# Attention, a routed mixture of experts and a dense layer on one core: the order of the products in the experts' second layer

## The chip, the cores and the metric

The kernel runs on one core of a Trainium2 chip. The metric is the device time of one execution in microseconds (us). The kernel before was timed in three runs; one more execution was taken by the hardware profiler.

## What is computed

Causal attention with a window of 64 positions over 4 batches, 8 heads, 576 positions and a head dimension of 64 gives N = 2304 tokens of 512 columns. A routed layer follows, and then a dense one:

```
skip_score = x @ w_skip;  do_compute = skip_score > 0
xc = x[do_compute]; e_idx = argmax(xc @ w_gate); gate_w = softmax(...)[e_idx]
for e in range(8):
    h = maximum(xc[e_idx == e] @ w1[e], 0)          # 512 -> 1024
    y[e_idx == e] = gate_w * (h @ w2[e])            # 1024 -> 512
out[do_compute] = xc + y
h2 = out @ w_in                                      # 512 -> 2048
g  = 0 if h2 <= -1 else h2 if h2 >= 1 else (h2+1)**2/4
return g @ w_out                                     # 2048 -> 512
```

## The kernel before

All products of the two layers are split products. A float32 operand v is kept as an upper half (ScalarE, ACT, rounds a copy) and a lower half (VectorE, DVE, subtracts the copy from v), and one product a*b becomes three matmuls: upper by upper, upper by lower, lower by upper. `PASSES = ((0, 0), (0, 1), (1, 0))` names the halves of the stationary and of the moving operand. The function `split` (lines 116 to 118) makes the halves of an activation: line 117 is ACT's upper half, line 118 DVE's lower half, which needs line 117 first. `split_pair` (lines 120 to 125) does the same for 1024 columns of weights, line 122 on ACT and line 123 on DVE.

Three stages follow each other: attention with the routing (to about 147 us of the span), the experts (to about 313 us), and the dense layer. The change touches the experts.

The expert stage works through the 8 experts in order. Expert e takes its tokens in tiles of 128 rows, gathered from the DRAM tile x1 by an indirect DMA that GpSimd (POOL) issues (`load_x`, line 650) and scattered back in the same way (`store_x`, line 657). The first tile of each expert is always computed; a second, a third and more only if the count of the expert asks for it (the branches of lines 774, 779 and 783). `prep` transposes a tile on TensorE (PE, line 665, four transposes) and splits it into mxT. `ffn` then does, for one tile:

- the first layer in two halves of 512 inner columns, `mm1` into the banks ha and hb (line 682). `mm1` has 12 products for a half, its 8 products with the upper half of mxT first, its 4 with the lower half last;
- `evac` (ACT, line 689) takes a half out of PSUM with the relu, `tr` transposes it on PE (line 695, four transposes into hTp) and splits it into hT. The first half's `tr` stands in the middle of hb's products;
- the second layer, 24 products into one bank y (line 720), 12 with the first half of the inner columns (j = 0), 12 with the second (j = 1). The second half's `tr` stands after the sixth of j = 0;
- line 726 on DVE: y times the gate plus the tile.

Within one j the kernel before goes over the four blocks c of 128 inner columns and does the three products of a block one after the other:

```
for c in range(4):
    ...
    for a, b in PASSES:
        nc.tensor.matmul(
            py, lhsT=hT[j][:, a, c, :], rhs=halves[4 * e + 2 + j, c][:, b, :],
```

so the third product of a half (c = 0, a = 1) is the first that reads the lower half of hT.

The weights of the next experts are loaded (SyncE's queue) and split while an expert is computed. Where this stands in the program is set by the hooks of `ffn` (lines 761 to 772): at "start", "a", "b" and before each block of j = 1 the function `work` issues the next weight splits, and hook 0 prepares the first tile of the next expert. So ACT and DVE have weight splits between the splits of mxT and hT, in the order of the program, and an engine takes its instructions in that order. POOL's queue alternates between gathers for later tiles and scatters of finished ones; both go to x1, and each scatter stands behind the gathers ahead of it and each gather behind the scatters ahead of it. The dense layer loads its rows from x1 after the last scatter; between the last tile and these rows PE does 28 matmuls whose results are not used (`keep_warm`, line 946).

Of the kernel before, what the change touches and what calls it, by code (L numbers as in the profile page):

```python
# [60 lines left out]
PASSES = ((0, 0), (0, 1), (1, 0))  # L61
# [3 lines left out]
def moe_chain(  # L65
# [10 lines left out]
    nc = tc.nc  # L76
# [11 lines left out]
    halves = {}  # L88
# [27 lines left out]
    def split(dst_hi, dst_lo, src):  # L116
        nc.scalar.activation(dst_hi, src, AF.Copy)  # L117
        nc.vector.tensor_tensor(dst_lo, src, dst_hi.bitcast(F32), ALU.subtract)  # L118
# [129 lines left out]
    with ExitStack() as actx:  # L248
# [308 lines left out]
        for t in range(NT):  # L557
# [19 lines left out]
            if t >= 5:  # L577
                t0, i, n, side = of[t - 5]
# [19 lines left out]
        t1, n = NT - ROUTES[-1], ROUTES[-1]  # L598
# [42 lines left out]
    with ExitStack() as ectx:  # L641
# [3 lines left out]
        def bank(i, shape, name):  # L645
            return psp.tile(shape, F32, tag=f"bank{i}", name=name)
# [23 lines left out]
        def ffn(e, x, xT, name, hooks=(), b0=0):  # L670

            hooks = dict(hooks)

            def at(k):
                if k in hooks:
                    hooks[k]()

            def mm1(ph, j, lo, hi):
                seq = [(c, a, b) for p in (PASSES[:2], PASSES[2:]) for c in range(KD) for a, b in p]
                for n in range(lo, hi):  # L680
                    c, a, b = seq[n]
                    nc.tensor.matmul(  # L682
                        ph, lhsT=xT[:, a, c, :], rhs=halves[4 * e + j, c][:, b, :],
                        start=(n == 0), stop=(n == len(seq) - 1),
                    )

            def evac(ph, j):
                h = mp.tile([P, 512], F32, tag="h", name=f"h{name}_{j}")
                nc.scalar.activation(h, ph, AF.Relu)
                return h  # L690

            def tr(h, j):
                pt = bank(b0 + j, [P, 4, P], f"hTp{name}_{j}")
                for c in range(4):
                    nc.tensor.transpose(pt[:, c, :], h[:, c * P : (c + 1) * P], ident)
                hT = mp.tile([P, 2, 4, P], F32R, tag=f"hT{j}", name=f"hT{name}_{j}", bufs=1)
                split(hT[:, 0], hT[:, 1], pt)
                return hT

            at("start")  # L700
            pa = bank(b0, [P, 512], f"ha{name}")
            mm1(pa, 0, 0, 12)
            ha = evac(pa, 0)
            pb = bank(b0 + 1, [P, 512], f"hb{name}")
            mm1(pb, 1, 0, 6)
            hTa = tr(ha, 0)
            at("a")
            mm1(pb, 1, 6, 12)
            hb = evac(pb, 1)
            py = bank(b0 + 2, [P, 512], f"y{name}")  # L710
            hT = [hTa, None]
            for j in range(2):
                for c in range(4):
                    if j == 0 and c == 2:
                        hT[1] = tr(hb, 1)
                        at("b")
                    if j == 1:
                        at(c)
                    for a, b in PASSES:
                        nc.tensor.matmul(  # L720
                            py, lhsT=hT[j][:, a, c, :], rhs=halves[4 * e + 2 + j, c][:, b, :],
                            start=(j == 0 and c == 0 and (a, b) == PASSES[0]),
                            stop=(j == 1 and c == 3 and (a, b) == PASSES[-1]),
                        )
            y = x[:, 0:DM]
            nc.vector.scalar_tensor_tensor(y, py, x[:, DM:RW], y, op0=ALU.mult, op1=ALU.add)

# [11 lines left out]
        def tile_of(e, t, hooks=()):  # L739
            ffn(e, xe[e, t], xeT[e, t], f"{e}_{t}", hooks, 4 if t else 0)  # L740
# [10 lines left out]
        for e in range(NE):  # L751
# [22 lines left out]
            with tc.If(counts[e] > P):  # L774
                pre(e, 1)
                fetch(e, 2)
                tile_of(e, 1)
                store_x(at_of(e, 1), xe[e, 1])
                with tc.If(counts[e] > 2 * P):  # L779
                    pre(e, 2)  # L780
                    tile_of(e, 2)
                    store_x(at_of(e, 2), xe[e, 2])
                    with tc.If(counts[e] > 3 * P):
                        with tc.For_i(0, (counts[e] - (2 * P + 1)) // P, 1) as i:
                            at = mp.tile([P, 1], I32, tag="at", name=f"at{e}", bufs=1)
                            nc.vector.tensor_copy(at, idx[:, bass.ds(i + (e * NT + 3), 1)])
                            x = load_x(at, f"{e}_l", "mxl", 1)
                            ffn(e, x, prep(x, f"{e}_l", "mxTl"), f"{e}_l", b0=4)
                            store_x(at, x)
# [282 lines left out]
```

## Time and profile before

| what | us |
|---|---|
| median of 3 runs | 749.52 |
| lowest and highest of the 3 | 745.4, 752.06 |
| the profiled execution | 744.33 |
| its span, first to last instruction | 742.6 |
| time of the profiled execution outside of the span | 1.73 |

The mean granted clock of TensorE over the span is 0.98 of full speed. Times in the rows below are us from the start of the span. PE is TensorE's matmul, PEld its weight load, DVE VectorE, ACT ScalarE, POOL GpSimd. The ends of matmuls are modelled: two matmuls that follow each other overlap in the rows, so the distance from one start to the next is the better measure.

### The profile page before, as it was taken

To read this page: it belongs to the slowest core of one execution; us is meant where nothing else is said; L and a number is where in the kernel's file an instruction comes from. 1 tells how busy PE (TensorE), PEld (TensorE's weight loads), DVE (VectorE), ACT (ScalarE), POOL (GpSimd) and SP (SyncE) were. 2 spreads that over 40 slices of the span, in tenths; PEclk is the share of its full clock that TensorE was granted. 3 is DMA by queue.
4 is the path that set the end of the run, shared out by engine and by line. 5 is a ranking of instruction groups with operands and counts; after the bars stand their busy time and mean duration, and the time that the engine had idled before them with its cause. 6 is when DMAs were issued, how large, how long until landed. Compare 5 with 4: busy or idle time off the path is not lost.

```text
span 742.6 us, 12124 instructions
## 1 busy us (share of the span) xinstructions
PE 682.9 (92%) x4605; PEld 581.4 (78%) x4605; DVE 432.9 (58%) x851; ACT 382.3 (51%) x761; POOL 95.1 (13%) x96
## 2 busy tenths in 40 slices
PE   7677887789798999799899999999999999999997
PEld 6565666667676777488798998999998998998995
DVE  4477776649759159679888874434343443333332
ACT  5654663027456257356676665545444544445443
POOL 2335554322022122100000000000000000000000
PEclk9987999999999999999999999999999999999999
DMA  8896965158949348354242400202030021002001
GB/s 262 261 280 199 288 197 144 31 172 265 334 134 350 115 126 297 135 172 142 87 142 86 128 1 0 72 15 72 15 86 1 1 44 43 1 0 44 1 1 43
DMA packets 34502, 88.81 MB, mean 120 GB/s; under 512 B 6958, under 2 KB 8110, under 8 KB 34420
## 3 DMA queue, kind: packets, MB, share of 16 engines
q1 hardware_dynamic: 26208, 74.34, 32.5%
q10 hardware_dynamic: 5892, 6.83, 2.8%
q0 software_dynamic: 2320, 6.58, 2.7%
q8 instruction: 47, 0.77, 0.4%
q14 instruction: 35, 0.29, 0.1%
HBM read 75.65 MB, written 13.12 MB: 120 GB/s over the span
## 4 chain that ended last, share of the span: by engine, by line
PE 47%; DVE 7%; DMA 3%; issue 2%; ACT 2%; ACTq 0%; POOLq 0%; DVEq 0%; SPq 0%
PE po L862 23%; PE h L833 23%; DVE c L855 2%; DMA x<-mx,idx 2%; ACT q L845 1%; DVE gs L853 1%; DVE w L123 1%; DVE c L852 1%; PE p2x L824 1%; DMA mx<-x,idx 1%; DVE q L844 1%; DVE x2T L118 0%; DVE q L848 0%; PE spare L946 0%; DVE c_first L855 0%
## 5 line engine op out<-in xcount | busy, mean ns | idle before, releaser
L833 PE MATMUL h<-x2T,w 128*128 128x384 f32 x1152 | 218.2, 337 | 4.3 <-ACT x2T L117 2.2
L862 PE MATMUL po<-w,gs 128*128 128x512 f32 x864 | 217.4, 395 | 0.7 <-DVE w L123 0.6
L833 PEld LDWEIGHTS h<-x2T,w 128*128 128x128 f32 x1152 | 204.6, 188 | 13.6 <-DVE x2T L118 2.7
L862 PEld LDWEIGHTS po<-w,gs 128*128 128x128 f32 x864 | 159.5, 188 | 31.2 <-DVE w L123 1.3
L841 ACT ACTIVATE q<-h 128x384 f32<-128x384 f32 x96 | 47.0, 489 | 109.7 <-PE h L833 108.3
L844 DVE TENSOR_SCALAR q<-q 128x384 f32<-128x384 f32 x96 | 34.3, 358 | 99.9 <-ACT q L841 99.6
L848 DVE TENSOR_TENSOR q<-hs,q 128x384 f32<-128x384 f32 x96 | 53.6, 559 | 49.5 <-ACT q L845 49.5
L850 ACT ACTIVATE gs<-q 128x384 fp32r<-128x384 f32 x96 | 50.4, 525 | 60.0 <-DVE q L848 60.0
L853 DVE TENSOR_TENSOR gs<-q,gs 128x384 fp32r<-128x384 f32 x96 | 53.6, 558 | 43.8 <-ACT gs L850 43.8
L720 PE MATMUL y<-w,hT 128*128 128x512 f32 x264 | 69.3, 402 | 4.9 <-DVE hT L118 4.9
L122 ACT ACTIVATE w<-raw 128x1024 fp32r<-128x1024 f32 x64 | 65.4, 1063 | 14.1 <-PEq L779 3.6
L845 ACT ACTIVATE q<-q 128x384 f32<-128x384 f32 x96 | 50.5, 526 | 23.3 <-DVE q L844 20.1
L720 PEld LDWEIGHTS y<-w,hT 128*128 128x128 f32 x264 | 47.7, 188 | 17.4 <-DVE hT L118 8.4
L123 DVE TENSOR_TENSOR w<-raw,w 128x1024 fp32r<-128x1024 f32 x50 | 58.9, 1218 | 2.6 <-ACT w L122 1.6
L323 ACT ACTIVATE pr<-s,nb 128x128 f32<-128x128 f32 x144 | 39.1, 386 | 29.4 <-DVE nb L319 29.4
L843 ACT ACTIVATE hs<-h 128x384 f32<-128x384 f32 x96 | 46.8, 488 | 0.0
L123 POOL TENSOR_TENSOR w<-raw,w 128x1024 fp32r<-128x1024 f32 x14 | 33.4, 2387 | 62.1 <-ACT w L122 62.1
L682 PE MATMUL ha<-w,mxT 128*128 128x512 f32 x132 | 34.0, 404 | 7.8 <-DVE mxT L118 3.3
L348 PE MATMUL o<-vt,pts 128*64 128x65 f32 x576 | 27.0, 250 | 12.4 <-DMA vt<-in_vs 11.1
L682 PEld LDWEIGHTS ha<-w,mxT 128*128 128x128 f32 x132 | 23.8, 188 | 17.1 <-DVE mxT L118 4.1
L348 PEld LDWEIGHTS o<-vt,pts 128*64 128x64 f32 x576 | 23.6, 160 | 16.3 <-DMA vt<-in_vs 10.8
L682 PE MATMUL hb<-w,mxT 128*128 128x512 f32 x132 | 35.0, 401 | 0.0
(159 smaller groups left out, 702.4 us busy)
## 6 DMA issues: line engine op xcount, KB each, us to landing
raw<-in_wu SPq DMA_DIRECT2D x62, 512.0 KB, 6.4
raw<-in_wd SPq DMA_DIRECT2D x32, 512.0 KB, 4.3
x<-x SPq DMA_DIRECT2D x20, 256.0 KB, 3.3
x<-x ACTq DMA_DIRECT2D x19, 256.0 KB, 5.8
vt<-in_vs SPq DMA_DIRECT2D x36, 130.0 KB, 5.6
out<-out SPq DMA_DIRECT2D x36, 128.0 KB, 2.4
q<-in_qs SPq DMA_DIRECT2D x8, 512.0 KB, 7.4
kt<-in_ks SPq DMA_DIRECT2D x8, 512.0 KB, 8.4
```

What stands on the lines that cost most here:

```text
L122: nc.scalar.activation(t[:, 0], src, AF.Copy)
L123: eng.tensor_tensor(t[:, 1], src, t[:, 0].bitcast(F32), ALU.subtract)
L348: nc.tensor.matmul(o[k * BLK : (k + 1) * BLK, h, 0:VW], lhsT=pts[k][:, h // 2, half * BLK : (half + 1) * BLK], rhs=vt[(2 * t + k) % B][:, ...
L682: nc.tensor.matmul(ph, lhsT=xT[:, a, c, :], rhs=halves[4 * e + j, c][:, b, :], start=(n == 0), stop=(n == len(seq) - 1),)
L720: nc.tensor.matmul(py, lhsT=hT[j][:, a, c, :], rhs=halves[4 * e + 2 + j, c][:, b, :], start=(j == 0 and c == 0 and (a, b) == PASSES[0]), s ...
L833: nc.tensor.matmul(ph, lhsT=halves[U_IN + m // 4, c][:, b, (m % 4) * P : (m % 4 + 1) * P], rhs=xT[:, a, c, :], start=(n == 0), stop=(n == ...
L841: nc.scalar.activation(q, ph, AF.Relu, bias=0.5, scale=0.5)
L845: nc.scalar.activation(q, q, AF.Square)
L848: nc.vector.tensor_tensor(q, h, q, ALU.max)
L850: nc.scalar.activation(gs[:, 0], q, AF.Copy)
L853: dve.tensor_tensor(gs[:, 1], q, gs[:, 0].bitcast(F32), ALU.subtract)
L862: nc.tensor.matmul(po[i], lhsT=gs[:, a, i * P : (i + 1) * P], rhs=w[:, b, :], start=(m == m0 and (a, b) == PASSES[0]), stop=(m == m1 - 1 a ...
```

## The change

In each half j the 12 products are put in the order that `mm1` has: first the 8 with the upper half of hT (a = 0) for c = 0 to 3, then the 4 with its lower half (a = 1). The second half's `tr` and hook "b" stay after the sixth product of j = 0, and the hooks 0 to 3 after the same numbers of products of j = 1 as before. The products, their operands and their sum are the same.

```diff
             hT = [hTa, None]
+
+            seq = [(c, a, b) for p in (PASSES[:2], PASSES[2:]) for c in range(4) for a, b in p]
             for j in range(2):
-                for c in range(4):
-                    if j == 0 and c == 2:
+                for n, (c, a, b) in enumerate(seq):
+                    if j == 0 and n == 6:
                         hT[1] = tr(hb, 1)
                         at("b")
-                    if j == 1:
-                        at(c)
-                    for a, b in PASSES:
-                        nc.tensor.matmul(
-                            py, lhsT=hT[j][:, a, c, :], rhs=halves[4 * e + 2 + j, c][:, b, :],
-                            start=(j == 0 and c == 0 and (a, b) == PASSES[0]),
-                            stop=(j == 1 and c == 3 and (a, b) == PASSES[-1]),
-                        )
+                    if j == 1 and n % 3 == 0:
+                        at(n // 3)
+                    nc.tensor.matmul(
+                        py, lhsT=hT[j][:, a, c, :], rhs=halves[4 * e + 2 + j, c][:, b, :],
+                        start=(j == 0 and n == 0), stop=(j == 1 and n == len(seq) - 1),
+                    )
```

On PE, the second layer of the first tile of expert 2 (hT_0_0 is the first half of the inner columns, hT_0_1 the second; w_0 and w_2 are weight tiles with the blocks c = 0, 1 and c = 2, 3; mpx is the next expert's tile that hook 0 prepares). Before:

```order
L720 MATMUL y_0_3411<-w_0_3034,hT_0_0_3385 128x512 x6
L695 MATMUL hTp_0_1_3418<-ident,h_0_1_3409 128x128 x4
L720 MATMUL y_0_3411<-w_2_3042,hT_0_0_3385 128x512 x6
L665 MATMUL mpx_0_3442<-ident,mx_0_2919 128x128 x4
L720 MATMUL y_0_3411<-w_0_3348,hT_0_1_3423 128x512 x6
L720 MATMUL y_0_3411<-w_2_3353,hT_0_1_3423 128x512 x6
```

With the change, the same place on PE:

```order
L721 MATMUL y_0_3411<-w_0_3034,hT_0_0_3385 128x512 x4
L721 MATMUL y_0_3411<-w_2_3042,hT_0_0_3385 128x512 x2
L695 MATMUL hTp_0_1_3418<-ident,h_0_1_3409 128x128 x4
L721 MATMUL y_0_3411<-w_2_3042,hT_0_0_3385 128x512 x2
L721 MATMUL y_0_3411<-w_0_3034,hT_0_0_3385 128x512 x2
L721 MATMUL y_0_3411<-w_2_3042,hT_0_0_3385 128x512 x2
L665 MATMUL mpx_0_3442<-ident,mx_0_2919 128x128 x4
L721 MATMUL y_0_3411<-w_0_3348,hT_0_1_3423 128x512 x4
L721 MATMUL y_0_3411<-w_2_3353,hT_0_1_3423 128x512 x4
L721 MATMUL y_0_3411<-w_0_3348,hT_0_1_3423 128x512 x2
L721 MATMUL y_0_3411<-w_2_3353,hT_0_1_3423 128x512 x2
```

The transposes of lines 695 and 665 stand after the same number of products as before; only the products of one half have changed places, so that the last four of each half are those with hT's lower half.

On DVE, the same tile, from the lower half of the second hT (line 118, hT_0_1) to the first layer of the expert's second tile (mxT_1). These rows are the same before and with the change, as are all rows of DVE, ACT, POOL and SyncE:

```order
L118 TENSOR_TENSOR hT_0_1_3423<-hTp_0_1_3418,hT_0_1_3423 128x512
L123 TENSOR_TENSOR w_2_3426<-raw_2_3010,w_2_3426 128x1024
L123 TENSOR_TENSOR w_0_3431<-raw_0_3032,w_0_3431 128x1024
L118 TENSOR_TENSOR mxT_0_3447<-mpx_0_3442,mxT_0_3447 128x512
L123 TENSOR_TENSOR w_2_3453<-raw_2_3037,w_2_3453 128x1024
L123 TENSOR_TENSOR w_0_3458<-raw_0_3045,w_0_3458 128x1024
L123 TENSOR_TENSOR w_2_3466<-raw_2_3351,w_2_3466 128x1024
L726 SCALAR_TENSOR_TENSOR mx_0_2451<-y_0_3411,mx_0_2451 128x512
L774 COMPARE_AND_BRANCH
L118 TENSOR_TENSOR mxT_1_3484<-mpx_1_3479,mxT_1_3484 128x512
```

Nothing moves here: five weight splits, mxT of the next expert and line 726 stand between the lower half of hT_0_1 and the lower half of mxT_1 in both kernels.

## Rows read from the trace of the kernel before

**Rows 1.** The page: the span, and busy time of each engine.
```profile
span 742.6 us, 12124 instructions
PE 682.9 (92%) x4605; PEld 581.4 (78%) x4605; DVE 432.9 (58%) x851; ACT 382.3 (51%) x761; POOL 95.1 (13%) x96
```
**Rows 2.** The page's groups: count, then busy us, mean ns, idle before.
```profile
L720 PE MATMUL y<-w,hT 128*128 128x512 f32 x264 | 69.3, 402 | 4.9 <-DVE hT L118 4.9
```
**Rows 3.** Waits from 150 to 312 us: total, times, longest.
```profile
PE y L720 <- DVE hT L118: 4.9, 8, 0.9
```
**Rows 4.** Timeline of PE at expert 2: start, us, instruction, idle before it.
```profile
184.87 0.62 PE L720 MATMUL y<-w,hT 128*128 128x512 f32 x2
186.13 1.20 PE L720 MATMUL y<-w,hT 128*128 128x512 f32 x4 [0.64 <-DVE hT L118]
...
189.35 0.72 PE L720 MATMUL y<-w,hT 128*128 128x512 f32 x2
190.92 2.57 PE L720 MATMUL y<-w,hT 128*128 128x512 f32 x10 [0.85 <-DVE hT L118]
...
194.61 2.12 PE L682 MATMUL ha<-w,mxT 128*128 128x512 f32 x8 [0.69 <-ACT mxT L117]
198.45 0.72 PE L682 MATMUL ha<-w,mxT 128*128 128x512 f32 x2 [1.72 <-DVE mxT L118]
```
**Rows 5.** Timeline of DVE in the same stretch.
```profile
185.39 0.68 DVE L118 TENSOR_TENSOR hT<-hTp,hT 128x512 fp32r<-128x512 f32 x1
...
190.18 0.68 DVE L118 TENSOR_TENSOR hT<-hTp,hT 128x512 fp32r<-128x512 f32 x1
...
197.72 0.68 DVE L118 TENSOR_TENSOR mxT<-mpx,mxT 128x512 fp32r<-128x512 f32 x1
```
**Rows 6.** Two stretches: length, busy us and instructions of each engine, PEclk, DMA share, GB/s.
```profile
169.57:198.40 28.83, 24.27 (x114) 18.30 (x112) 27.29 (x33) 18.91 (x24) 4.63 (x4) 1.00 0.90 310
219.33:241.40 22.07, 18.57 (x84) 13.66 (x82) 21.74 (x25) 14.91 (x19) 5.43 (x4) 1.00 0.92 322
```
**Rows 7.** Timeline of PE at the second tile of expert 4.
```profile
241.44 1.20 PE L682 MATMUL ha<-w,mxT 128*128 128x512 f32 x4 [1.55 <-DVE mxT L118]
```
**Rows 8.** Timeline of PE at experts 6 and 7: two sets of 12 products.
```profile
279.26 3.04 PE L682 MATMUL ha<-w,mxT 128*128 128x512 f32 x12
...
289.85 3.01 PE L720 MATMUL y<-w,hT 128*128 128x512 f32 x12
```
**Rows 9.** DMA issues from 283.5 to 285 us: the gather of 283.87, us to landing.
```profile
mx<-x,idx POOLq DMA_INDIRECT x1, 8.2
```
**Rows 10.** The chain that ended last, from 292 us: start, us, what.
```profile
292.89 6.62 DMA x<-mx,idx
...
300.44 4.62 DMA mx<-x,idx
...
305.84 3.37 DMA x<-mx,idx
...
310.12 2.66 DMA x<-mx,idx
```
**Rows 11.** Timeline of DVE: line 726 of the last tile.
```profile
306.01 0.75 DVE L726 SCALAR_TENSOR_TENSOR mx<-y,mx 128x512 f32<-128x512 f32 x1 [0.16 <-PE y L720]
```
**Rows 12.** Timeline of PE in attention, and at the start of the dense layer.
```profile
53.00 0.33 PE L348 MATMUL o<-vt,pts 128*64 128x65 f32 x2 [1.88 <-DMA vt<-in_vs]
...
54.73 1.97 PE L333 MATMUL pt<-ident,pr 128*128 128x128 f32 x8
...
61.63 1.09 PE L333 MATMUL pt<-ident,pr 128*128 128x128 f32 x8
...
315.99 0.30 PE L824 MATMUL p2x<-ident,x 128*128 128x128 f32 x1 [2.82 <-DMA x<-x]
```
**Rows 13.** Stretches, columns as in rows 6.
```profile
54.38:57.79 3.41, 3.41 (x27) 2.39 (x27) 1.75 (x4) 0.60 (x1) 1.96 (x1) 0.50 1.04 314
...
194.32:201.15 6.83, 4.82 (x21) 3.65 (x22) 4.07 (x5) 0.84 (x2) 0.00 (x0) 1.00 0.95 310
...
317.20:320.61 3.41, 3.41 (x13) 1.92 (x12) 2.55 (x4) 2.40 (x4) 0.00 (x0) 0.50 0.75 259
```

## The prediction

> **What bounds the kernel now.** I read the page first, then the groups and the waits of the expert stage, then the timelines of PE, DVE and POOL through it, and at last the chain that ended last. PE is the busiest engine by far [rows 1], but the share is an average over three stages, and the change touches only the expert stage. There the changed line has 264 products, 24 for each of 11 computed tiles, and PE's idle time just before them is 4.9 us [rows 2]. All of it is eight waits for the lower half of hT, the longest 0.9 us [rows 3]. So at most eight of 22 halves wait at all.
>
> The reader should then look at who is late. At expert 2 PE does two products, waits for line 118, and does the rest; this happens in both halves, and further on the first layer of the expert's second tile waits 1.72 us, again for line 118 [rows 4]. DVE's rows show why: the lower halves of hT start at 185.39 and 190.18 with no idle time before them, and the lower half of mxT at 197.72 has none either [rows 5]. DVE is busy for 27.29 of 28.83 us from 169.57 to 198.40, and for 21.74 of 22.07 us from 219.33 to 241.40 [rows 6]; it is working off weight splits. PE is released from the second stretch in the same way, after 1.55 us, at 241.44 [rows 7]. In these two stretches DVE sets the time, not the order of PE's products.
>
> The end of the stage is set by something else again. From 292.89 the chain that ended last is scatter, gather, scatter, scatter, one after the other [rows 10]. The scatter at 292.89 stands behind the gather issued at 283.87, which lands 8.2 us later, at 292.07 [rows 9]. The last tile is finished by DVE at 306.01 + 0.75 = 306.76 [rows 11], but its scatter starts only at 310.12 [rows 10]: the tile lies there for 3.4 us because the scatter before it has not landed.
>
> **What the change does to PE, step by step.** The pitch of the products: 12 of them take 3.01 us [rows 8] with a mean of 0.402 us for one [rows 2], so (3.01 - 0.40) / 11 = 0.24 us from start to start. Before, the lower half had to be there after two products, 0.48 us into a half. Now it has eight, 1.9 us, and for j = 0 also the four transposes in between.
>
> What each wait costs PE by starts: at j = 1 of expert 2 it is 190.92 - 189.35 - 0.48 = 1.09 us where the row says 0.85, at j = 0 it is 186.13 - 184.87 - 0.48 = 0.78 where it says 0.64 [rows 4]. The modelled end of a product hides 0.14 to 0.24 us, so the eight waits are worth about 4.9 + 8 x 0.19 = 6.4 us of PE's time. Taken alone each is shorter than the 1.4 us of new slack, so as long as nothing else moves, they all go.
>
> The price of the new order itself: line 682 already works in this order, and its 12 products take 3.04 us against 3.01 us in the old order [rows 8]. The bounds are thus 0 and 22 x 0.03 = 0.7 us; a gain from the order alone is excluded, since products, shapes and operands stay. I take 0. No DMA, no split and no wait of another engine is moved, so nothing has to be costed on the queues of ACT, DVE, POOL and SyncE.
>
> What of the 6.4 us reaches the end:
>
> (The parts are counted by starts, as above, and add up to 6.4.)
>
> - Expert 1's second half and both halves of expert 2 hold three of the waits, 0.8 + 0.8 + 1.1 = 2.7 us. They lie in the stretch in which DVE never rests, and its order is unchanged, so the lower half of mxT still comes at 197.72 + 0.68 = 198.40 and PE goes on at 198.45. Gain: 0. Since PE now comes early to j = 1, it still waits there until 190.9, but with four products behind it instead of ten; so it arrives 6 x 0.24 = 1.4 us earlier at the first layer of the second tile, and the wait of 1.72 us becomes about 3.2 us.
> - Two of expert 4's waits, 1.5 us, lie in the second such stretch. Gain: 0. The 1.55 us at 241.44 grow by 0.7 us (ACT's weight splits let no more through) to the full 1.5 us; I take 2.3 us.
> - The last three, 2.2 us at experts 5 to 7, come after DVE's queue has drained, so PE does get ahead. But the scatters do not: the tile is ready 1.5 to 2.2 us earlier and lies 5 to 5.6 us instead of 3.4. Gain: 0, with bounds of -1.3 us (if the scatter at 292.89 waits for DVE's split that ends just there, and not for the gather) and +0.5 us (weight loads that start earlier beside a scatter).
>
> So the sum by work is 0, and what is left is PE's clock. In rows at 0.50 the engine had been idle shortly before: 1.88 us idle at 53.00 [rows 12], then the stretch from 54.38 at 0.50, the lower level of 1.2 GHz [rows 13]; 2.82 us idle at 315.99 [rows 12], then 317.20 to 320.61 at 0.50 [rows 13]. The wait of 1.72 us at expert 2 was not followed by a fall: 194.32 to 201.15 stands at 1.00, 2.4 GHz [rows 13]. The two waits that the change lengthens come to 3.2 and 2.3 us, at or past the gaps that were followed by one. Between the two stretches of rows 6, and for as long after the second, PE sets the time, so a fall is paid in full. Its price: eight transposes of line 333 took 1.97 us at the lower level against 1.09 us [rows 12], 0.9 us for these alone; a whole stretch of 3.41 us at 0.50 [rows 13] loses half of itself, 1.7 us, if PE is busy throughout. I take 1.5 us for one, and one more such stretch than before: 1.5 us.
>
> The Trainium skill, TensorE: Matmul & The Clock Gate, section "Loop structure matters more than you think", speaks against the change: matmuls that stand behind a long wait run cold, so the same idle time in one piece is dearer than in several. This trace agrees with its 1.88 and 2.82 us gaps; by the rule both lengthened waits fall, which is the slower rival below, and without it the sum would be 0.
>
> The sum against the profiled execution: 744.33 + 0 + 1.5 = 745.8 us, of which the span is 742.6 and 1.73 us lie outside. The median of the runs is 749.52, 5.19 us above the profiled execution, and the new time is measured as the old one was, so I forecast 745.8 + 5.2 = 751.0 us.
>
> **The rivals.**
>
> - No cost at all: the waits go, DVE and the scatters swallow them, and the clock stays as it was (or falls in as many places as in the runs before, which already differ by 6.7 us among themselves). For it: a 1.72 us wait that did no harm. Time: 749.5 us.
> - The gain comes through. For it: PE is at 92% of the span [rows 1], and the chain goes back from the scatter at 292.89 to DVE's split of mxT. Against it: rows 5, 6 and 9. If only that link holds, 749.5 - 1.3 = 748.2; if everything passed, 749.5 - 6.4 = 743.1 us. The nearer end is the likelier.
> - Slower: the collected wait at expert 2, that at expert 4 and the gap before the dense layer all cost a stretch. The mechanism is PE's idle time in one piece: PE waits 3.2 us at 198 and 2.3 us at 241, and at the end it runs out of filler matmuls 1.6 to 2.2 us earlier, so that the gap of 2.82 us grows to 4.4 to 5. Price: 1.5 + 1.5 us for the first two and 0.6 us at the end, where PE has only a few transposes to do at the lower level, together 3.6 us, 753.1 us. It decides from the point at which a gap between 1.72 and 2.3 us is already too long.
>
> That the change does not do what it says is excluded by the order of PE's rows.
>
> **How the numbers follow.** One more stretch at the lower clock (751.0): 0.45. No cost (749.5): 0.20. The gain comes through (743.1 to 748.2, mostly the latter): 0.15. Two or three stretches (752.5 to 753.1, and more where a run falls badly): 0.20. The runs before spread from 745.4 to 752.06, so each case is blurred by about 3 us. The range from 745.0 to 757.0 leaves out most of the complete gain below, and of the slower case only what lies beyond its price and that blur. A change of 1%, 7.5 us, is about what a measurement of this kernel can tell from none. Even the complete gain of 6.4 us is less than that, and so is the slower case, 3.6 us. Only with the blur on top is it crossed: faster by over 1% 0.03, within 1% 0.94, slower by over 1% 0.03.
>
> **What would show it.** In the profile after, PE's idle time before the products of y should fall from 4.9 to 1 to 2 us, with a wait left between the eighth and the ninth product at j = 1 of expert 2. The waits of the first layer for mxT should grow from 1.72 and 1.55 to about 3.2 and 2.3 us, with DVE as busy as before in the same stretches and line 118 of mxT ending at about 198.4 and 241.4, moved only by what the clock cost before. PEclk should show one or two stretches at 0.50 between 195 and 250 that were not there. Line 726 of the last tile should come earlier against the last scatter, and the last scatter should start at 310 plus the clock's cost. I am wrong if the first load of the dense layer comes over 1 us earlier than 312.8 (then DVE or PE, not the scatters, set the end), if mxT of expert 2's second tile ends earlier than 198 us, or if the products themselves take longer than 0.24 us each in the new order.

## The result, and the profile after

| | before | after |
|---|---|---|
| median us (runs) | 747.13 (22) | 750.96 (22) |
| lowest, highest | 739.2, 752.06 | 747.08, 756.17 |
| ratio, 95% interval | | 1.0073, 1.0052 to 1.0093 |
| profiled execution, its span | 744.33, 742.6 | 747.08, 745.4 |

The change makes the kernel slower by 0.73%: 5.4 us of 747.13, or 3.9 to 6.9 by the interval. The ratio compares runs on the same chip; the two medians, which do not, stand 3.8 us apart. That is less than the 1% of the forecast's bounds, but it is clear of noise.

The page after has the same number of instructions, and the waits before the products of y have nearly gone. The idle time before the first layer (line 682) has grown instead, from 7.8 to 11.0 us. First its row before (columns as in [rows 2]), then the page after:

```profile
L682 PE MATMUL ha<-w,mxT 128*128 128x512 f32 x132 | 34.0, 404 | 7.8 <-DVE mxT L118 3.3
```
```profile
span 745.4 us, 12124 instructions
PE 689.6 (93%) x4605; PEld 588.0 (79%) x4605; DVE 432.4 (58%) x851; ACT 383.2 (51%) x761; POOL 94.2 (13%) x96
...
L721 PE MATMUL y<-w,hT 128*128 128x512 f32 x264 | 67.6, 399 | 1.2 <-DVE hT L118 1.2
...
L682 PE MATMUL ha<-w,mxT 128*128 128x512 f32 x132 | 36.4, 425 | 11.0 <-DVE mxT L118 4.9
```

Against [rows 2], PE's idle time before y fell from 4.9 to 1.2 us. Its products take 399 ns where they took 402, so the order itself costs nothing. PE as a whole is 6.7 us busier than in [rows 1] with the same instructions: the products of line 682 take 425 ns on average where they took 404. The timeline of PE shows which ones, at expert 2 and at the second tile of expert 4 (it answers to [rows 4] and [rows 7]):

```profile
184.32 1.54 PE L721 MATMUL y<-w,hT 128*128 128x512 f32 x6
...
187.97 2.09 PE L721 MATMUL y<-w,hT 128*128 128x512 f32 x8
191.23 1.21 PE L721 MATMUL y<-w,hT 128*128 128x512 f32 x4 [1.17 <-DVE hT L118]
...
193.74 2.12 PE L682 MATMUL ha<-w,mxT 128*128 128x512 f32 x8 [0.86 <-ACT mxT L117]
198.76 1.19 PE L682 MATMUL ha<-w,mxT 128*128 128x512 f32 x4 [2.90 <-DVE mxT L118]
199.79 2.61 PE L682 MATMUL hb<-w,mxT 128*128 128x512 f32 x6
...
243.30 1.24 PE L682 MATMUL ha<-w,mxT 128*128 128x512 f32 x4 [2.00 <-DVE mxT L118]
244.34 2.76 PE L682 MATMUL hb<-w,mxT 128*128 128x512 f32 x6
```

The two stops at the third product have become one, behind the eighth, and the wait for mxT has grown from 1.72 to 2.90 us at expert 2 and from 1.55 to 2.00 at expert 4. Behind each, six products take 2.61 and 2.76 us; before, the same six took 1.54:

```profile
199.48 1.54 PE L682 MATMUL hb<-w,mxT 128*128 128x512 f32 x6
...
242.48 1.54 PE L682 MATMUL hb<-w,mxT 128*128 128x512 f32 x6
```

The stretches of the trace with PEclk, the granted clock of TensorE as a share of full speed (columns as in [rows 6]), give the reason:

```profile
199.96:203.37 3.41, 3.41 (x11) 2.73 (x11) 0.00 (x0) 0.62 (x2) 0.00 (x0) 0.50 0.98 359
...
244.33:247.74 3.41, 3.41 (x12) 2.72 (x10) 0.00 (x0) 0.60 (x1) 0.43 (x1) 0.50 0.89 362
169.90:198.70 28.80, 23.78 (x114) 18.31 (x112) 27.30 (x33) 18.90 (x24) 4.29 (x4) 1.00 0.90 305
221.60:243.30 21.70, 17.95 (x83) 13.38 (x81) 21.32 (x25) 14.50 (x19) 5.94 (x4) 1.00 0.92 318
```

Both stretches behind the waits stand at 0.50, 1.2 GHz. Before, PEclk stayed at 1.00 there, at expert 2 by [rows 13] and at expert 4 by this row:

```profile
238.69:245.52 6.83, 5.28 (x26) 4.03 (x25) 3.04 (x5) 1.19 (x2) 0.06 (x1) 1.00 0.97 363
```

The last two rows of the trace after are the stretches of [rows 6]: DVE is busy for 27.30 of 28.80 and for 21.32 of 21.70 us, as before. Its lower half of mxT comes as late as before, although PE came earlier to the first layer (193.74 against 194.61):

```profile
197.37 0.74 DVE L726 SCALAR_TENSOR_TENSOR mx<-y,mx 128x512 f32<-128x512 f32 x1
198.03 0.68 DVE L118 TENSOR_TENSOR mxT<-mpx,mxT 128x512 fp32r<-128x512 f32 x1
```

It ends at 198.71 against 198.40 in [rows 5]; the first product of expert 1 lies 0.28 us later here as well (165.39 against 165.11). The end of the stage, in the chain that ended last (it answers to [rows 10]), and the last line 726 (to [rows 11]):

```profile
296.71 6.09 DMA x<-mx,idx
...
303.74 4.10 DMA mx<-x,idx
...
308.62 2.84 DMA x<-mx,idx
...
312.38 2.67 DMA x<-mx,idx
```
```profile
307.57 0.75 DVE L726 SCALAR_TENSOR_TENSOR mx<-y,mx 128x512 f32<-128x512 f32 x1
```

The last scatter again starts about 4 us after its tile is finished (308.32, 312.38): scatter, gather, scatter and scatter stand in line as before.

A measure that leaves attention and the dense layer out is the time from the first product of expert 1 to the first product of expert 5. Before it is 265.61 - 165.11 = 100.50 us, after 269.06 - 165.39 = 103.67. The difference of 3.2 us lies where the two stretches at the lower clock lie: the tile after each wait takes longer by 1.56 us (from 198.45 to 209.28, and from 198.76 to 211.15) and by 1.6 us.

### The profile page after: what moved, and what is told of

Same layout as the page of the kernel before. It is cut to its first block, busy times and chain, and to the rows that moved or that the text cites. A ratio compares the mean times of both kernels' runs of the same rounds, so it can differ in the third digit from the quotient of the medians.

```text
span 745.4 us, 12124 instructions
## 1 busy us (share of the span) xinstructions
PE 689.6 (93%) x4605; PEld 588.0 (79%) x4605; DVE 432.4 (58%) x851; ACT 383.2 (51%) x761; POOL 94.2 (13%) x96
## 4 chain that ended last, share of the span: by engine, by line
PE 52%; DMA 6%; DVE 4%; issue 1%; ACT 1%; POOLq 0%; DVEq 0%; SPq 0%; ACTq 0%
PE po L862 25%; PE h L833 25%; DMA x<-mx,idx 3%; DMA mx<-x,idx 2%; PE p2x L824 1%; DVE c L855 1%; DMA x<-x 1%; DVE gs L853 1%; ACT q L845 1%; DVE w L123 0%; DVE c L852 0%; PE ha L682 0%; DVE c_first L855 0%; DVE q L844 0%; DVE q L848 0%
## 5 line engine op out<-in xcount | busy, mean ns | idle before, releaser
L850 ACT ACTIVATE gs<-q 128x384 fp32r<-128x384 f32 x96 | 50.4, 525 | 60.0 <-DVE q L848 60.0
L721 PE MATMUL y<-w,hT 128*128 128x512 f32 x264 | 67.6, 399 | 1.2 <-DVE hT L118 1.2
L682 PE MATMUL ha<-w,mxT 128*128 128x512 f32 x132 | 36.4, 425 | 11.0 <-DVE mxT L118 4.9
L682 PEld LDWEIGHTS ha<-w,mxT 128*128 128x128 f32 x132 | 25.4, 201 | 20.9 <-DVE mxT L118 5.8
L682 PE MATMUL hb<-w,mxT 128*128 128x512 f32 x132 | 37.8, 424 | 0.0
L118 DVE TENSOR_TENSOR hT<-hTp,hT 128x512 fp32r<-128x512 f32 x22 | 15.1, 687 | 37.7 <-ACT hT L117 30.1
```

Of the source, the lines that this page charges most:

```text
L682: nc.tensor.matmul(ph, lhsT=xT[:, a, c, :], rhs=halves[4 * e + j, c][:, b, :], start=(n == 0), stop=(n == len(seq) - 1),)
L721: nc.tensor.matmul(py, lhsT=hT[j][:, a, c, :], rhs=halves[4 * e + 2 + j, c][:, b, :], start=(j == 0 and n == 0), stop=(j == 1 and n == len ...
L850: nc.scalar.activation(gs[:, 0], q, AF.Copy)
```

## The experiments

The theory: the waits are gathered into one long wait behind DVE's queue, PE's clock falls behind it, and the end of the stage swallows the rest. Rival A: the new order is dearer on PE. Rival B: DMA timing at the end of the stage. The table gives the measure just named, the waits for mxT at experts 2 and 4 in the trace ("-" for none), and the ratio to the kernel before on the same chip with its 95% interval. The experiments ran on three chips, A, B and C, on which the median of before was 747.61, 743.46 and 743.25, so only ratios are compared.

| kernel | chip | expert 1 to 5, us | waits for mxT, us | ratio |
|---|---|---|---|---|
| before | | 100.50 | 1.72, 1.55 | |
| before again | B | 100.55 | 1.72, 1.72 | 1.0004 (0.9972 to 1.0037) |
| after | | 103.67 | 2.90, 2.00 | 1.0073 (1.0052 to 1.0093) |
| after again | C | 102.02 | 3.10, 0.40 | 1.0072 (1.0029 to 1.0114) |
| new order in j = 0 only | A | 100.23 | 1.73, 1.31 | 1.0011 (0.9986 to 1.0036) |
| new order in j = 1 only | A | 102.87 | 2.16, - | 1.0034 (1.0010 to 1.0057) |
| new order, filler in all experts | A | 100.27 | 0.70, - | 1.0033 (1.0004 to 1.0062) |
| new order, filler in experts 2 and 4 | B | 101.10 | 1.35, - | 1.0049 (1.0017 to 1.0081) |
| old order, filler in experts 2 and 4 | C | 100.77 | -, - | 1.0047 (1.0023 to 1.0072) |
| old order, conversions moved | B | 99.03 | 0.79, - | 0.9994 (0.9960 to 1.0027) |
| the same, second chip | C | 99.01 | 0.80, - | 0.9997 (0.9967 to 1.0027) |
| new order, conversions moved | A | 98.95 | 0.86, - | 0.9950 (0.9919 to 0.9980) |
| the same, second chip | C | 99.85 | 0.85, - | 0.9965 (0.9934 to 0.9997) |
| the same, longer fillers at two gaps | B | 97.66 | 0.79, - | 1.0055 (1.0024 to 1.0085) |

**One half at a time.** The order of each half is chosen apart:

```diff
+            old = [(c, a, b) for c in range(4) for a, b in PASSES]
-                for n, (c, a, b) in enumerate(seq):
+                for n, (c, a, b) in enumerate(old if j else seq):    # j = 0 only
+                for n, (c, a, b) in enumerate(seq if j else old):    # j = 1 only
```

> Only the first half's products (j = 0) are in the new order. Theory (the collected wait makes PE's clock fall): at expert 2 and expert 4 PE still stops at the third product of j = 1 until about 190.9 and 233.9 us, so the waits of the second tiles' first layer stay at about 1.7 and 1.6 us, no stretch at 0.50 is added and the time is that of before, ratio 0.997 to 1.003. Rival A (the new order itself is dearer on PE): about half of the loss of 3.9 to 7 us, ratio 1.003 to 1.005. Rival B (DMA timing at the end of the expert stage): a change of either sign up to 1.5 us, with no change at 198 and 241 us.

> Only the second half's products (j = 1) are in the new order. Theory (collected wait and clock): at expert 2 the four products behind the wait give the same 1.4 us of lead as the whole change, at expert 4 about 0.7 us, so both waits of the second tiles' first layer are as long as with the whole change (about 2.9 and 2.0 us), the clock falls behind them, and the ratio is that of the whole change, 1.004 to 1.009. Rival A (the order itself): half of the loss, 1.003 to 1.005. Rival B (DMA timing): no relation to the waits.

With the new order in j = 0 alone the ratio holds no change clear of noise, and the two waits are not longer (1.73 and 1.31 us). With the new order in j = 1 alone the loss is there, about half of it by the ratio where I had expected all of it; by this ratio alone it could be rival A's. The trace of its PE shows this at experts 2 and 4:

```profile
201.88 1.45 PE L682 MATMUL ha<-w,mxT 128*128 128x512 f32 x4 [2.16 <-DVE mxT L118]
...
242.69 0.63 PE L665 MATMUL mpx<-ident,mx 128*128 128x128 f32 x4 [2.11 <-DMA mx<-x,idx]
244.01 4.42 PE L682 MATMUL ha<-w,mxT 128*128 128x512 f32 x12 [0.69 <-ACT mxT L117]
```

At expert 4 it is not DVE but the gather of the second tile that PE now waits for, 2.11 us, and the 12 products behind that take 4.42 us in place of 3.04. So a wait for something other than DVE can be followed by the fall too. The two halves hold the same products in the same two orders, so a dearer order would have shown in j = 0 as well, with 1.003 to 1.005 where 1.0011 was measured. That interval still touches rival A's range; the products of y, which take 399 ns in place of 402, speak against it as well. Rival A falls.

**Filler in the waits.** Eight matmuls whose results are not used stand behind the eighth product of the second tile's first layer, first in all experts, then in experts 2 and 4 alone, and at last with the old order as a control:

```diff
-            mm1(pa, 0, 0, 12)
+            mm1(pa, 0, 0, 8)
+            if name in ("2_1", "4_1"):            # first version: name[2:] == "1"
+                fill = bank(b0 + 1, [P, 512], f"fill{name}")
+                for _ in range(8):
+                    nc.tensor.matmul(fill, lhsT=ones, rhs=..., start=True, stop=True)
+            mm1(pa, 0, 8, 12)
```

> The changed kernel with 8 more matmuls of 128x512 whose results are not used, on the second tile of an expert alone, between the products of the first layer that need mxT's upper half and those that need its lower half; some 1.8 us of PE, inside the waits of 2.9 and 2.0 us. Theory (clock): PEclk stays at 1.00 from 190 to 260 us, line 118 of mxT still ends at about 198.7 and 241.4, and the loss goes: 3 us less than the changed kernel, ratio to before 0.997 to 1.002. Rival A (the order itself) and rival B (DMA timing): the filler changes nothing, ratio 1.005 to 1.009.

> As the filler kernel before (8 matmuls inside the wait of the second tile's first layer), but the filler stands only in experts 2 and 4, so that the skipped blocks of the other experts keep their size. Theory (clock, and the wait of 4 us on PE's sequencer behind the branch of expert 5 in the filler kernel came from the larger skipped blocks): no stretch at 0.50 from 190 to 260 us, no wait of several us behind a branch, the loss of the changed kernel goes by about 3 us, ratio 0.998 to 1.003. Rival A (the order itself): ratio 1.005 to 1.009. Rival C (filler of any kind costs PE time): ratio as with the first filler, 1.003.

> A control for the filler: the kernel before, old order, with the same 8 unused matmuls in experts 2 and 4 inside the wait of the second tile's first layer (1.7 and 1.6 us, which they fill). Theory (a filler inside a wait is free there, and what the filler kernels lost came from elsewhere, from the scatters or from instructions that lie in other places): expert 1 to expert 5 in 100.5 us plus at most 0.5, the time 0.998 to 1.005 of before. If it comes out at 1.003 or more, the filler itself costs about what the filler kernel with the new order lost, and that kernel does not speak for another loss of the new order.

In the stage the filler does what the theory says: the new order with filler takes 100.27 and 101.10 us from expert 1 to expert 5, 2.6 to 3.4 us less than without it in the first trace, and 0.9 to 1.8 us less than in the second (102.02). The stretch from 190 to 260 us of the second version, and its PE at expert 2:

```profile
190.00:260.00 70.00, 62.58 (x293) 47.73 (x292) 43.98 (x52) 32.89 (x44) 10.73 (x10) 1.00 0.68 242
```
```profile
198.69 1.90 PE L706 MATMUL fill<-ones 128*128 128x512 bf16 x8
201.94 1.20 PE L682 MATMUL ha<-w,mxT 128*128 128x512 f32 x4 [1.35 <-DVE mxT L118]
202.97 1.54 PE L682 MATMUL hb<-w,mxT 128*128 128x512 f32 x6
```

PEclk is 1.00 throughout, and the six products behind the wait take 1.54 us again. But the whole kernel did not come back to the time of before, although I had expected that of both versions: the filler has a price of its own. The control measures it: the old order with the same filler is at 1.0047. Between the two kernels with filler, the order makes 0.0002; between the two without, 0.0073. So the loss of the new order hangs on PE being idle at those two places. The two kernels with filler ran on different chips, each beside before, and their intervals together leave some 0.4% to either side (my estimate); where the filler's own 0.47% lies was not found; the window itself holds 0.3 us of it (100.77 against 100.50). In the first version, where the filler stands in the skipped blocks of experts 5 and 6 as well, one part can be seen, a wait of PE's sequencer behind the branch of line 774 (782 in that kernel):

```profile
286.63 5.46 PE L682 MATMUL ha<-w,mxT 128*128 128x512 f32 x12 [4.04 <-PEq L782]
```

The two kernels with filler in experts 2 and 4 alone show no such wait.

**Less work in DVE's queue.** Two of the conversions for the dense layer's weights move away from experts 2 and 4, by the table that deals them out:

```diff
-SLOW = (2, 4, 5, 6, 6, 7, 8, 8, 8)
+SLOW = (2, 4, 5, 5, 6, 6, 7, 8, 8)
```

> The changed kernel, and two of the dense layer's weight conversions (5 DVE instructions, 2.9 us each) moved from expert 2 to expert 3 and from expert 4 to 5 and 5 to 6. Theory (DVE's queue swallows the gain in the two stretches): mxT of expert 2's second tile ends about 2.9 us earlier, PE's wait there falls from 2.9 to under 0.5 us, that at expert 4 from 2.0 to under 1 us, no stretch at 0.50 between 190 and 260 us, and the second half's gain comes through: 4 to 6 us less than before, ratio 0.992 to 0.996. Rival (the scatters and gathers set the end of the expert stage whatever comes before): the third tile of expert 4 ends earlier, but the dense layer's rows are not loaded earlier than at about 312 us, ratio 0.999 to 1.002.

> The kernel before with the two weight conversions moved away from experts 2 and 4 as in the relief kernel, and the products in the old order. It tells what of the relief kernel's 0.5% belongs to the order. Theory (DVE's queue set the time in the two stretches): the move alone gives part, PE still stops at third products; the new order is worth 1 to 4 us on top of it, so this ratio lies between 0.996 and 1.000. Rival (the move does everything, the new order is worth nothing even without the queue): ratio 0.993 to 0.996.

> The relief kernel (new order, two conversions moved) beside the next one on one chip. Theory: expert 1 to expert 5 in about 99 us or less; the wait for DVE is gone, what is left is the gather of expert 4's second tile, about 2.4 us, behind which the clock falls in some runs. Ratio 0.993 to 0.999.

> The two conversions moved, old order, beside the kernel ahead of it. Theory (with DVE's queue shortened the next limit is the gather, so the new order is worth little): within 0.3% of the relief kernel with the new order, ratio 0.995 to 1.001. Rival (the new order is worth its 2 to 4 us once DVE is relieved): 0.3 to 0.5% slower than the relief kernel with the new order.

The move shortens PE's wait at expert 2 from 2.90 to 0.86 us (expected: under 0.5), and with it the new order is faster than before: 0.9950 and 0.9965, against 0.9994 and 0.9997 with the old order. Both samples point the same way by 0.3 to 0.4%, 2 to 3 us, but the intervals of a pair still overlap, and the first pair ran on two chips; the two differences taken together are 0.4% with some 0.3% to either side (my estimate). Neither the move alone nor the order alone makes the kernel faster. The expectation for the first pair (the order worth 1 to 4 us) was met. In the last pair the difference of 0.32% lies on the border between the theory (the order worth little, under 0.3%) and its rival, and does not decide. No stretch at the lower clock was expected from 190 to 260 us, but there is one. In the trace of the new order with the move, PE's next limit is the gather of expert 4's second tile:

```profile
238.01 1.09 PE L665 MATMUL mpx<-ident,mx 128*128 128x128 f32 x4 [2.43 <-DMA mx<-x,idx]
239.78 5.18 PE L682 MATMUL ha<-w,mxT 128*128 128x512 f32 x12 [0.69 <-ACT mxT L117]
```

2.43 us of idle time, and 12 products in 5.18 us behind it: the same loss once more, at another wait. With it the stage is as long as with the old order (98.95 and 99.03 us) in these two traces; in the second pair, with 3.16 us of idle time there, it is longer (99.85 and 99.01 us). So no trace shows where the 2 to 3 us of the ratio are gained: the two profiled executions with the new order took 747.81 and 746.25 us, those with the old one 743.40 and 741.85.

**Longer fillers at two gaps.**

```diff
-KEEP = (24, 26, 56, 6, 8, 28)
+KEEP = (24, 26, 88, 6, 8, 36)
```

> The relief kernel (new order, two conversions moved) with longer fillers in two gaps of PE: 88 in place of 56 matmuls of 128x128 before the first gather of the expert stage, 36 in place of 28 of 128x512 before the dense layer's rows. Theory (what is left to lose is the clock behind PE's idle gaps): the stretches at 0.50 near 148 and near 319 us go, ratio 0.988 to 0.994, 1 to 3 us below the relief kernel. Rival (these gaps are covered by DMA and the clock there costs nothing): ratio of the relief kernel, 0.995.

A miss. The stretches at the lower clock near 148 and 319 us did go, and the time from expert 1 to expert 5 is the shortest of all, 97.66 us. One reason lies at expert 4:

```profile
230.83 0.63 PE L665 MATMUL mpx<-ident,mx 128*128 128x128 f32 x4 [2.54 <-DMA mx<-x,idx]
232.15 3.03 PE L682 MATMUL ha<-w,mxT 128*128 128x512 f32 x12 [0.69 <-ACT mxT L117]
```

PE waits for the gather a little longer than in the kernel without the longer fillers (2.43 us), and yet its 12 products take 3.03 us and not 5.18: this time the clock did not fall. But expert 5 to the dense layer's first transpose took 56.7 us, 6.3 more than before, and the trace shows why:

```profile
274.31 3.85 PE L682 MATMUL ha<-w,mxT 128*128 128x512 f32 x9 [2.45 <-issue]
...
291.39 4.53 PE L682 MATMUL ha<-w,mxT 128*128 128x512 f32 x12 [3.61 <-PEq L774]
```

PE stands still for 2.45 us behind the third product of expert 6, and its sequencer comes 3.61 us late out of that expert's skipped block, where nothing was lost before. Of the unused matmuls that were added, only the 32 ahead of the expert stage lie ahead of these places. Why they have this effect was not found.

**Both kernels once more.**

> The kernel before once more, for a second trace. Theory (the whole change adds low stretches behind the two lengthened waits): the waits of the second tiles' first layer are about 1.7 and 1.6 us again, at most one stretch at 0.50 between 190 and 260 us. The stretches outside of that window (attention, the first gather of the expert stage near 148 us, near 317 and 360 us) may differ from the first trace of before by several, since the kernels tried so far all show one near 148 and one near 360 that the first trace of before lacks. Rival: those two are there only with the new order, so they would be missing here again.

> The changed kernel once more, beside the next three on one chip. Theory: from the start of expert 1 to the start of expert 5 it takes about 103.7 us against 100.5 us before, with a stretch at 0.50 behind each of the two lengthened waits; the mean granted clock of its runs lies 0.004 to 0.007 below that of the runs of before, and the ratio is 1.004 to 1.008. Rival (the two stretches are an accident of one trace): 100.5 us and no stretch between 190 and 260 us.

The second trace of before repeats the stage to 0.05 us, with no stretch at 0.50 between 190 and 260 us. It does have the stretches near 151 and 356 us that the first one lacked, so these belong to no change. The second trace of after has two falls again, at 193.07 and 234.03 us:

```profile
193.11 2.07 PE L682 MATMUL ha<-w,mxT 128*128 128x512 f32 x4 [3.10 <-DVE mxT L118]
...
232.39 0.63 PE L665 MATMUL mpx<-ident,mx 128*128 128x128 f32 x4 [1.09 <-DMA mx<-x,idx]
233.70 3.52 PE L682 MATMUL ha<-w,mxT 128*128 128x512 f32 x8 [0.69 <-ACT mxT L117]
237.62 1.19 PE L682 MATMUL ha<-w,mxT 128*128 128x512 f32 x4 [0.40 <-DVE mxT L118]
```

The first lies behind the long wait as in the first trace. The second does not: it comes ahead of the wait for DVE, behind 1.09 us for the gather and 0.69 us for ACT. The eight products that it slows down fill what would have been a wait for DVE (0.40 us is left of it), so it costs nothing: hence 102.02 us and not 103.67. The clock of the runs points the same way for many executions: on that chip the mean granted clock is 0.9651 with the change and 0.9747 before, a larger drop than I had expected (0.004 to 0.007), and (1 - clock) times the mean time is 26.1 and 18.8 us. The 7.3 us between them are some four stretches of 3.41 us at half speed [rows 13], 1.7 us each. Two of them can be those at experts 2 and 4; where the others lie was not found. This sum is not a loss of time: by the same reckoning the two profiled executions of before, at a clock of 0.980 and 0.971, differ by 6.7 us (14.9 and 21.6), and their spans by 1.8.

## Why the prediction was right and wrong

- Right: PE does not gain in the stretches where DVE never rests. The lower half of mxT stayed in its place, the wait behind the eighth product at expert 2 came where it was expected, and the two lengthened waits came to 2.9 and 2.0 us in the first trace (forecast 3.2 and 2.3). In the second the one at expert 2 came to 3.1 us; at expert 4 the slow products left only 0.4.
- Right in the main: the end of the stage does not follow the lead of experts 5 to 7. Line 726 of the last tile stands 38.5 us after the start of expert 5 in both traces of after (40.4 before). The dense layer's first transpose stands at 49.3 and 52.4 us (50.4 and 50.6 before). The lead is there; counted from expert 5, the end came 1.0 us earlier in the one trace and 2.0 us later in the other, which is outside the prediction's bounds of -1.3 and +0.5 us. The same link of the chain, a scatter, landed after 6.1 us in the one and 8.9 in the other.
- Right: the new order has no price on PE (399 against 402 ns, and j = 0 alone at 1.0011).
- Wrong in size: "I take 1.5 us for one, and one more such stretch than before." The price of a stretch was right, 1.6 us each; the count was not. In the first trace of after both lengthened waits were followed by a fall, 3.2 us together; in the second the one at expert 2 was, and the fall at expert 4 cost nothing. Two falls paid are the main part of the slower rival, put at 0.20, and its 3.6 us lie nearer to the measured 3.9 to 6.9 us than my 1.5. I had rows that spoke for it: falls had followed gaps of 1.88 and 2.82 us [rows 12], so a wait put at 2.3 us deserved a chance of one as well as one of 3.2. It was no certainty: a gap of 2.22 us at 355.17 in the same trace was not followed by a fall.
- The third place of that rival, the gap before the dense layer, grew from 2.82 us to 3.68 in the first traces (forecast 4.4 to 5) and from 3.04 to 6.82 in the second, and a low stretch lies there in both traces of after. Of before, one trace has it and one has not.
- The time of 751.0 us was met (750.96) by accident: the three runs that I started from had a median of 749.52, the 22 runs one of 747.13, so the start was 2.4 us too high and the loss that I added, 1.5 us, too low by as much between the medians (3.8) and by more in the ratio (5.4).
- The signs named at the end of the prediction are met in the first trace of after: mxT at 198.71 and the first load of the dense layer at 315.26 us, neither of them early. In the second trace expert 1 starts 5.7 us earlier than in the first, so times counted from the start of the span tell nothing there.

Shown: a part of the loss arises behind the collected waits at experts 2 and 4, 3.2 us in one trace and 1.5 in the other, and with PE kept busy there the ratios show no difference between the orders, to within 0.4%. Still open: what makes the measured 5.4 us larger than that. The gap before the dense layer and the scatters (rival B) are candidates, and no run told them apart. The end of the stage is not neutral: from expert 5 to the dense layer's first transpose the five traces with the old order (with filler or moved conversions or neither) take 50.1 to 50.6 us, with the new order the two of after and the one with filler in experts 2 and 4 take 49.3, 52.4 and 52.6 us, the two with moved conversions 50.6.

The only version that is faster than before by its interval on both chips is the new order with the two conversions moved: 0.9950 and 0.9965 of before.

## What to carry to other kernels

Before removing a wait, find out who is late. If the engine waited for is saturated, an earlier start only carries the idle time to its next wait, and several short pauses become one long one, which on TensorE can cost a stretch at half clock on top. Together with two conversions of some 3 us each moved out of the late engine's queue, the same edit came out 0.35 to 0.5% faster than before, where neither did alone; so an edit that loses alone may be worth trying again once the late engine is relieved.

## What was not expected of the hardware

- At experts 2 and 4, gaps of 2.0 to 3.1 us on PE were followed by a fall to half clock in the traces of after, gaps of 1.55 and 1.72 us in those of before were not. But the length of one gap does not decide it: 2.54 us at expert 4 (longer fillers) and 3.04 us before the dense layer (second trace of before, the row below) were not followed by one, while 1.09 and 0.69 us close together were (second trace of after, expert 4).

```profile
316.27 0.63 PE L824 MATMUL p2x<-ident,x 128*128 128x128 f32 x4 [3.04 <-DMA x<-x]
```

- A fall whose slow products only fill a wait that follows cost nothing; one that was paid in full cost 1.6 us.
- Unused matmuls that stand elsewhere changed what a branch costs. With 32 more of them ahead of the expert stage, PE came 3.6 us late out of a skipped block, with 8 more in the second tile of every expert 4.0 us; before, its wait behind a branch is 0.43 us at most. The Trainium skill, Advanced Engine Details and Errata, section "ISA Cache", says that instructions are held in a few large lines; no run here shows whether the place of the branch in them is the cause.
- Near the end of the expert stage, scatters of a tile landed after 2.7 to 9.8 us; no run shows what makes the difference.
